# Strassen's scheme for half of the gate and up projections, with attention slices emitted at a higher pace

## The chip, the cores and the metric

The kernel runs on one core of one Trainium2 chip. The metric is the device time of one execution in microseconds (us). The span, from the first to the last instruction in a profile, is about 1.8 us shorter than the time of the same execution. In the profile lines PE is TensorE, PEld its weight loads, DVE VectorE, ACT ScalarE, POOL GpSimd, and SPq the queue of SyncE. PSUM holds the sums that matmuls build up, in 8 tiles (banks) in this kernel; an evacuation copies such a tile out.

## The reference

The input is x, 2048 tokens by 1024. Two blocks follow each other, each with a residual and a layer norm before it: a local attention with 32 heads of 32 (each token looks at 8 tokens, two apart), and a gated feed-forward block without an activation function.

```python
h  = x + A(layernorm(x), wqkv, wo)
# B: D = 1024, F = 3584
g = einsum("bsd,df->bsf", layernorm(h), w_gate)
u = einsum("bsd,df->bsf", layernorm(h), w_up)
h2 = h + einsum("bsf,fd->bsd", g * u, w_down)
```

## The kernel before

The tokens are cut into four chunks of 512. TensorE does all projections in bf16. VectorE does the attention, which has no matmul in it: for each of 8 offsets it multiplies and adds tiles of 128x4096. The attention is a generator, cut into slices. The program feeds slices into VectorE's instruction stream at a pace that a counter sets: each TensorE group earns credit, each slice costs some.

```python
class Background:
    def step(self, us):
        self.now += us
        self.credit = min(self.credit + us * self.rate, 4.0)
        while self.credit > 0:
            ...                              # next slice of a ready generator
            self.credit -= got               # (cut)
    def finish(self, gen):                   # emit all that is left of it, now
        ...
```

The attention's output goes through memory to be transposed: VectorE leaves it in `oD`, a store puts it in `od`, and four loads bring it back as `oT`.

```python
        nc.gpsimd.dma_start(od[c].rearrange("c g d s -> (c g) d s"), oD[:])
        oT = att.tile([128, KO, 4, SUB], BF, tag="oT", name=f"oT{c}")
        for cp in range(4):
            nc.gpsimd.dma_start(oT[:, :, cp, :], od[c][cp].rearrange("(hg hl) d s -> (hl d) hg s", hl=4))
```

The output projection (`wo`) reads `oT`. The feed-forward block has gate and up (`ffn1`) and the down projection (`ffn2`, two halves of 512 output columns):

```python
    def mm_group(ps, wt, j, rhs):            # ps: a PSUM tile
        for ko in range(KO):                 # 8 matmuls of 128x512
            nc.tensor.matmul(ps[:], lhsT=wt[:, ko, bass.ts(j, 128)], rhs=rhs[:, ko, :], ...)

    def ffn1(c, lnT):                        # (cut: loads, tiles)
        for b in range(7):
            for j in range(4):
                mm_group(pg, wts["wg", c, b], j, lnT)
                nc.scalar.copy(gs[:], pg[:])
                mm_group(pu, wts["wu", c, b], j, lnT)
                nc.scalar.copy(us[:], pu[:])
                nc.vector.tensor_tensor(gs[:], gs[:], us[:], ALU.mult)
```

The order at the end of the program:

```python
    qkv(3, range(4), last=True)
    bg.finish(atts[0])
    bg.rate = 0.9
    nxt = wo_ln2(0)
    qkv(3, range(4, 6), last=True)
    start_attention(3)
    for c in range(NCH):
        lnT2, hs = nxt
        hT = ffn1(c, lnT2)
        if c + 1 < NCH:
            bg.finish(atts[c + 1])
            nxt = wo_ln2(c + 1)              # output projection and layer norm
        ffn2(c, hT, hs)
```

## Time and profile before

| | kernel before |
|---|---|
| time, first three runs | 821.02, 824.99, 826.96 us |
| span of the profiled run | 817.9 us |
| TensorE busy | 99%, granted clock 1.00 |
| VectorE busy | 58%, but 81 to 98% in each stage from 20 us until the attention ends at 500 us |
| pace of a 128x512 bf16 matmul | 215.8 ns |
| attention of chunk 3 leaves VectorE | 499.85 us |
| its output projection starts | 607 us |

TensorE is the bound; the lines that show this stand in the prediction.

### The profile page before, as it was taken

To read this page: it belongs to the slowest core of one execution; us is meant where nothing else is said; L and a number is where in the kernel's file an instruction comes from. 1 tells how busy PE (TensorE), PEld (TensorE's weight loads), DVE (VectorE), ACT (ScalarE), POOL (GpSimd) and SP (SyncE) were. 2 spreads that over 40 slices of the span, in tenths; PEclk is the share of its full clock that TensorE was granted. 3 is DMA by queue.
4 is the path that set the end of the run, shared out by engine and by line. 5 is a ranking of instruction groups with operands and counts; after the bars stand their busy time and mean duration, and the time that the engine had idled before them with its cause. 6 is when DMAs were issued, how large, how long until landed. Compare 5 with 4: busy or idle time off the path is not lost.

```text
span 817.9 us, 9732 instructions
## 1 busy us (share of the span) xinstructions
PE 806.0 (99%) x3808; PEld 373.7 (46%) x3881; DVE 470.5 (58%) x520; ACT 222.4 (27%) x505; POOL 31.2 (4%) x60
## 2 busy tenths in 40 slices
PE   7999999999999999999999999999999999999998
PEld 5444444444444444444444444444444444444445
DVE  4539999998888899968887995111124111111011
ACT  2545444323333310023333000333320003333100
POOL 3100000200000200000200002000000000000000
PEclk9999999999999999999999999999999999999999
DMA  9999864999845969755863688636456753535400
GB/s 309 318 207 241 160 192 114 260 265 276 283 135 169 289 174 305 241 168 185 272 215 123 126 263 269 206 109 198 150 179 160 229 188 125 185 117 170 146 26 26
DMA packets 194494, 158.98 MB, mean 194 GB/s; under 512 B 83472, under 2 KB 188048, under 8 KB 192400
## 3 DMA queue, kind: packets, MB, share of 16 engines
q1 hardware_dynamic: 189904, 133.19, 57.4%
q0 software_dynamic: 4544, 25.17, 9.2%
q8 instruction: 30, 0.49, 0.3%
q14 instruction: 16, 0.13, 0.1%
HBM read 128.97 MB, written 22.02 MB: 185 GB/s over the span
## 4 chain that ended last, share of the span: by engine, by line
PE 97%; DMA 1%; issue 1%; SPq 0%; DVE 0%; ACT 0%
PE pg L330 24%; PE pu L330 24%; PE acc L512 21%; PE ps L330 19%; PE wo L453 7%; PE accl L502 3%; DMA x<-in_A_x_dram 1%; SPq L213 0%; PE ps L297 0%; SPq L221 0%; PE pt L288 0%; ACT lnT L289 0%; DVE ln L170 0%; DVE h L493 0%; DVE lnT L292 0%
## 5 line engine op out<-in xcount | busy, mean ns | idle before, releaser
L330 PE MATMUL pg<-lnT,w_wg 128*128 128x512 bf16 x879 | 210.1, 379 | 0.9
L330 PE MATMUL pu<-lnT,w_wu 128*128 128x512 bf16 x877 | 209.8, 379 | 0.9
L512 PE MATMUL acc<-w_wd,gs 128*128 128x512 bf16 x768 | 169.0, 379 | 0.8
L484 DVE TENSOR_TENSOR gs<-gs,us 128x512 bf16<-128x512 bf16 x112 | 47.4, 423 | 198.7 <-ACT us L483 198.7
L330 PE MATMUL ps<-lnT,w_qkv 128*128 128x512 bf16 x721 | 158.4, 379 | 0.8
L330 PEld LDWEIGHTS <-w_wg 128*128 128x128 bf16 x896 | 87.7, 98 | 105.7
L330 PEld LDWEIGHTS <-w_wu 128*128 128x128 bf16 x896 | 87.7, 98 | 105.7
L478 ACT CAST gs<-pg 128x512 bf16<-128x512 f32 x112 | 65.6, 586 | 235.9 <-PE pg L330 231.4
L512 PEld LDWEIGHTS <-gs 128*128 128x128 bf16 x784 | 76.7, 98 | 92.5
L330 PEld LDWEIGHTS <-w_qkv 128*128 128x128 bf16 x736 | 72.0, 98 | 86.6
L483 ACT CAST us<-pu 128x512 bf16<-128x512 f32 x112 | 65.6, 586 | 123.8 <-PE pu L330 114.6
L249 ACT CAST sg<-ps 128x512 bf16<-128x512 f32 x96 | 55.4, 586 | 63.8 <-PE ps L330 58.7
L415 DVE TENSOR_TENSOR pv<-vD,at 128x4096 bf16<-128x4096 bf16 x32 | 72.4, 2287 | 0.4
L375 DVE TENSOR_TENSOR prod<-qD,kD 128x4096 bf16<-128x4096 bf16 x32 | 72.3, 2285 | 0.1
L493 DVE TENSOR_TENSOR h<-acc,h 128x512 bf16<-128x512 f32 x28 | 17.4, 683 | 78.4 <-PE acc L512 78.4
L453 PE MATMUL wo<-w_wo,oT 128*128 128x512 bf16 x251 | 55.6, 379 | 0.3
L453 PEld LDWEIGHTS <-oT 128*128 128x128 bf16 x256 | 25.1, 98 | 30.2
L377 DVE TENSOR_TENSOR prod<-prod 128x4096 bf16<-128x4096 bf16 x16 | 36.6, 2289 | 0.3
L165 ACT ACTIVATE rs<-mv,eps 128x1 f32<-128x1 f32 x32 | 9.4, 294 | 75.7 <-DVE mv L162 70.8
L423 DVE TENSOR_TENSOR pv<-pv 128x4096 bf16<-128x4096 bf16 x12 | 27.5, 2289 | 0.2
L425 DVE TENSOR_TENSOR oD<-oD,pv 128x4096 bf16<-128x4096 bf16 x12 | 27.4, 2287 | 0.2
L502 PE MATMUL accl<-w_wd,gs 128*128 128x512 bf16 (+1 forms) x139 | 24.4, 336 | 0.1
(56 smaller groups left out, 291.3 us busy)
## 6 DMA issues: line engine op xcount, KB each, us to landing
w_wg<-in_B_w_gate_dram SPq DMA_DIRECT2D x28, 1024.0 KB, 7.0
w_wu<-in_B_w_up_dram SPq DMA_DIRECT2D x28, 1024.0 KB, 5.4
w_wd<-in_B_w_down_dram SPq DMA_DIRECT2D x32, 896.0 KB, 6.2
w_wo<-in_A_wo_dram SPq DMA_DIRECT2D x8, 1024.0 KB, 6.8
kd<-sg SPq DMA_DIRECT2D x32, 144.0 KB, 3.0
vd<-sg SPq DMA_DIRECT2D x32, 144.0 KB, 3.7
kD<-kd POOLq DMA_DIRECT2D x4, 1152.0 KB, 7.7
vD<-vd POOLq DMA_DIRECT2D x4, 1152.0 KB, 11.1
```

What stands on the lines that cost most here:

```text
L249: nc.scalar.copy(sg[:, HB:HB + TC], ps[:])
L330: nc.tensor.matmul(ps[:], lhsT=wt[:, ko, bass.ts(j, 128)], rhs=rhs[:, ko, :], start=(ko == 0), stop=(ko == KO - 1))
L375: nc.vector.tensor_tensor(prod[:, j], qD[:], kD[:, :, o:o + SUB], ALU.mult)
L377: nc.vector.tensor_tensor(prod[:, :, 0:16], prod[:, :, 0:16], prod[:, :, 16:32], ALU.add)
L415: nc.vector.tensor_tensor(pv[:, j], vD[:, :, o:o + SUB], at[:, w, None, :].to_broadcast((128, DH, SUB)), ALU.mult)
L423: nc.vector.tensor_tensor(pv[:, 0], pv[:, 0], pv[:, 1], ALU.add)
L453: nc.tensor.matmul(ps[:], lhsT=oTs[c][:, kk, t, :], rhs=wts["wo", c, hf][:, kk, :], start=(kk == 0), stop=(kk == KO - 1))
L478: nc.scalar.copy(gs[:], pg[:])
L483: nc.scalar.copy(us[:], pu[:])
L484: nc.vector.tensor_tensor(gs[:], gs[:], us[:], ALU.mult)
L502: nc.tensor.matmul(acc[:], lhsT=hT[f][:, bass.ts(t, 128)], rhs=wts["wd", c, hf, f // 7][:, f % 7, bass.ds(lo, n)], start=(f == 0), stop=(f ...
L512: nc.tensor.matmul(acc[t][:], lhsT=hT[f][:, bass.ts(t, 128)], rhs=wts["wd", c, hf, b][:, j, :], start=(f == 0), stop=(f == NF - 1))
```

## The change

The intent is to save matmuls. Chunks 2 and 3 are projected together, so that each pair of weight tiles meets a 2x2 arrangement: two halves of the contraction by two chunks. One level of Strassen's scheme (in Winograd's form) does this with 7 products in place of 8, for sums of weights and activations that other engines form. The sums are written as float32r, a four-byte type. Since chunks 2 and 3 are now needed together, chunk 3's attention has to be done much earlier, so its pace goes from 0.9 to 0.98.

```diff
+F32R = mybir.dt.float32r
...
+    def weight_sums(n, i):                       # GpSimd, per block and matrix
+        sw = wpool.tile([128, 4, 4, 128], F32R, tag="w", name=f"sw_{n}_{i}")
+        nc.gpsimd.tensor_tensor(sw[:, 0], a21, a22, ALU.add)
+        nc.gpsimd.tensor_tensor(sw[:, 1], sw[:, 0], a11, ALU.subtract)
+        nc.gpsimd.tensor_tensor(sw[:, 2], a11, a21, ALU.subtract)
+        nc.gpsimd.tensor_tensor(sw[:, 3], a12, sw[:, 1], ALU.subtract)
+        nc.scalar.copy(wc[:], a22)
...
+    def activation_sums(l2, l3):                 # once, on VectorE
+        nc.vector.tensor_tensor(t1[:], b12, b11, ALU.subtract)
+        ...
+    def product(ps, lhs, rhs, fresh):
+        for ko in range(4):
+            nc.tensor.matmul(ps[:], lhsT=lhs[:, ko, :], rhs=rhs[:, ko, :], start=(fresh and ko == 0),
+                             stop=(ko == 3), skip_group_check=not fresh)
...
+        for i in gu:                             # pair_block: gate and up (cut: PSUM tiles)
+            product(xb[i], wt[:, 0:4, i, 0:128], b11, True)      # bf16
+            nc.scalar.copy(yb[i][:], xb[i][:])                   # PSUM to PSUM
+        for i in gu:
+            product(vb[i], sw[i][:, 0], t1, True)                # float32r
+            nc.scalar.copy(p5[i][:], vb[i][:])
+            product(yb[i], sw[i][:, 1], t2, False)               # float32r
+            nc.scalar.copy(zb[i][:], yb[i][:])
+        for i in gu:
+            product(zb[i], sw[i][:, 2], t3, False)               # float32r
+            nc.vector.tensor_tensor(out[i][3], zb[i][:], p5[i][:], ALU.add)
+            product(xb[i], wt[:, 4:8, i, 0:128], b21, False)     # bf16
+            nc.scalar.copy(out[i][0], xb[i][:])
+        for i in gu:
+            product(zb[i], pair["c", n, i], t4, False)           # float32r
+            nc.scalar.copy(out[i][2], zb[i][:])
+            product(yb[i], sw[i][:, 3], bc, False)               # float32r
+            nc.vector.tensor_tensor(out[i][1], yb[i][:], p5[i][:], ALU.add)
+        for k in (3, 0, 2, 1):
+            nc.vector.tensor_tensor(out[0][k], out[0][k], out[1][k], ALU.mult)
...
-    bg.rate = 0.9
+    bg.rate = 0.98
...
+    hT = ffn1(1, lnT2)
+    bg.finish(atts[2])
+    l2, hs2 = wo_ln2(2)
+    h3 = att.tile([128, 4, D], BF, tag="qD", name="h3")          # residual of chunk 3
+    nc.sync.dma_start(h3[:], x[bass.ts(3, TC), :].rearrange("(t p) d -> p t d", p=128))
+    ffn2(1, 0, hT, hs)
+    bg.finish(atts[3])
+    l3, hs3 = wo_ln2(3)
+    activation_sums(l2, l3)                                      # (cut: loads, first weight_sums)
+    ffn2(1, 1, hT, hs, {0: lambda: weight_sums(0, 1)})
+    for n in range(NP):                                          # 14 blocks (cut)
+        pair_block(n, h23[4 * n:4 * n + 4])
+    # then the down projections of chunks 2 and 3
```

More of the change, by code (lines that the diff above doesn't have):

```diff
@@ L28 @@
 NF = F // 128
+NP = NF // 2
 EPS = 1e-5
@@ L127, with stream_wo, stream_wd @@
         stream.append((("qkv", b), wqkv_v[:, :, bass.ts(b, 512)], KO))
-    for c in range(NCH):
+    def stream_wo(c):
         for hf in range(2):
             stream.append((("wo", c, hf), wo_v[:, :, bass.ts(hf, 512)], KO))
+    def stream_wd(c, hf):
+        for b in range(4):
+            stream.append((("wd", c, hf, b), wd_v[:, bass.ts(b, 7), bass.ts(hf, 512)], 7))
+    for c in range(2):
+        stream_wo(c)
         if c > 0:
-            for hf in range(2):
-                for b in range(4):
-                    stream.append((("wd", c - 1, hf, b), wd_v[:, bass.ts(b, 7), bass.ts(hf, 512)], 7))
+            stream_wd(0, 0)
+            stream_wd(0, 1)
         for b in range(7):
@@ L137 @@
             stream.append((("wu", c, b), wu_v[:, :, bass.ts(b, 512)], KO))
-    for hf in range(2):
-        for b in range(4):
-            stream.append((("wd", NCH - 1, hf, b), wd_v[:, bass.ts(b, 7), bass.ts(hf, 512)], 7))
+    stream_wo(2)
+    stream_wd(1, 0)
+    stream_wo(3)
+    stream_wd(1, 1)
+    pair_at = len(stream)
+    for c in (2, 3):
+        stream_wd(c, 0)
+        stream_wd(c, 1)
     wts = {}
-    state = {"next": 0, "live": 0}
+    state = {"next": 0, "live": 0, "limit": pair_at}
     def pump(eng=None):
-        while state["next"] < len(stream) and state["live"] < 7:
+        while state["next"] < state["limit"] and state["live"] < 7:
             key, src, n = stream[state["next"]]
@@ L494, in ffn2_store @@
         nc.sync.dma_start(outf[bass.ds(c * TC + t * 128, 128), cols], hs[t][:, cols])
-    def ffn2(c, hT, hs):
-        for hf in range(2):
-            if c == NCH - 1 and hf == 1:
-                for t, lo, n in ((0, 0, 512), (1, 0, 512), (2, 0, 512), (3, 0, 256), (3, 256, 256)):
-                    acc = psum.tile([128, n], F32, tag="mm", name=f"accl{t}_{lo}")
-                    for f in range(NF):
-                        nc.tensor.matmul(acc[:], lhsT=hT[f][:, bass.ts(t, 128)],
-                                         rhs=wts["wd", c, hf, f // 7][:, f % 7, bass.ds(lo, n)],
-                                         start=(f == 0), stop=(f == NF - 1))
-                    ffn2_store(c, t, hf, acc, hs, lo, n)
-                continue
-            acc = [psum.tile([128, 512], F32, tag="mm", name=f"acc{c}_{hf}_{t}") for t in range(4)]
-            for b in range(4):
-                for j in range(7):
-                    f = b * 7 + j
-                    for t in range(4):
-                        nc.tensor.matmul(acc[t][:], lhsT=hT[f][:, bass.ts(t, 128)],
-                                         rhs=wts["wd", c, hf, b][:, j, :],
-                                         start=(f == 0), stop=(f == NF - 1))
-                    bg.step(0.86)
-                retire()
-            for t in range(4):
-                ffn2_store(c, t, hf, acc[t], hs)
-                bg.spend(0.7)
@@ new lines, in ffn2 @@
+    def ffn2(c, hf, hT, hs, between={}):
+        if c == NCH - 1 and hf == 1:
+            for t, lo, n in ((0, 0, 512), (1, 0, 512), (2, 0, 512), (3, 0, 256), (3, 256, 256)):
+                acc = psum.tile([128, n], F32, tag="mm", name=f"accl{t}_{lo}")
+                for f in range(NF):
+                    nc.tensor.matmul(acc[:], lhsT=hT[f][:, bass.ts(t, 128)],
+                                     rhs=wts["wd", c, hf, f // 7][:, f % 7, bass.ds(lo, n)],
+                                     start=(f == 0), stop=(f == NF - 1))
+                ffn2_store(c, t, hf, acc, hs, lo, n)
+            return
+        acc = [psum.tile([128, 512], F32, tag="mm", name=f"acc{c}_{hf}_{t}") for t in range(4)]
+        for b in range(4):
+            for j in range(7):
+                f = b * 7 + j
+                for t in range(4):
+                    nc.tensor.matmul(acc[t][:], lhsT=hT[f][:, bass.ts(t, 128)],
+                                     rhs=wts["wd", c, hf, b][:, j, :],
+                                     start=(f == 0), stop=(f == NF - 1))
+                bg.step(0.86)
+            retire()
+            if b in between:
+                between[b]()
+        for t in range(4):
+            ffn2_store(c, t, hf, acc[t], hs)
+            bg.spend(0.7)
@@ new lines, with load_pair @@
+    pair = {}
+    def load_pair(n):
+        wt = wpool.tile([128, KO, 2, 256], BF, tag="w", name=f"w_pair_{n}")
+        for i, src in enumerate((wg_v, wu_v)):
+            nc.sync.dma_start(wt[:, :, i, :], src[:, :, bass.ts(n, 256)])
+        pair["w", n] = wt
+        state["live"] += 1
+    def weight_sums(n, i):
+        wt = pair["w", n]
+        a11, a12 = wt[:, 0:4, i, 0:128], wt[:, 4:8, i, 0:128]
+        a21, a22 = wt[:, 0:4, i, 128:256], wt[:, 4:8, i, 128:256]
+        sw = wpool.tile([128, 4, 4, 128], F32R, tag="w", name=f"sw_{n}_{i}")
[3 more added lines that the diff above has]
+        nc.gpsimd.tensor_tensor(sw[:, 3], a12, sw[:, 1], ALU.subtract)
+        wc = lnp.tile([128, 4, 128], F32R, tag="ln", name=f"wc_{n}_{i}")
+        nc.scalar.copy(wc[:], a22)
+        pair["s", n, i], pair["c", n, i] = sw, wc
+        state["live"] += 1
@@ new lines, in activation_sums @@
+    def activation_sums(l2, l3):
+        b11, b12, b21, b22 = l2[:, 0:4, :], l3[:, 0:4, :], l2[:, 4:8, :], l3[:, 4:8, :]
+        t1 = att.tile([128, 4, TC], F32R, tag="kD", name="t1p")
+        t2 = att.tile([128, 4, TC], F32R, tag="vD", name="t2p")
+        t34 = att.tile([128, 2, 4, TC], F32R, tag="prod", name="t34p")
+        bc = att.tile([128, 4, TC], F32R, tag="oD", name="bcp")
+        nc.scalar.copy(bc[:], b22)
+        nc.vector.tensor_tensor(t1[:], b12, b11, ALU.subtract)
+        nc.vector.tensor_tensor(t2[:], b22, t1[:], ALU.subtract)
+        nc.vector.tensor_tensor(t34[:, 0], b22, b12, ALU.subtract)
+        nc.vector.tensor_tensor(t34[:, 1], b21, t2[:], ALU.subtract)
+        pair["b"] = (b11, b21, t1, t2, t34[:, 0], t34[:, 1], bc)
@@ new lines, in product, with pair_block, bank @@
+    def product(ps, lhs, rhs, fresh):
+        for ko in range(4):
+            nc.tensor.matmul(ps[:], lhsT=lhs[:, ko, :], rhs=rhs[:, ko, :], start=(fresh and ko == 0),
+                             stop=(ko == 3), skip_group_check=not fresh)
+    def pair_block(n, hts):
+        b11, b21, t1, t2, t3, t4, bc = pair["b"]
+        wt = pair["w", n]
+        gu = range(2)
+        sw = [pair["s", n, i] for i in gu]
+        out = [hts, [t1k.tile([128, TC], BF, tag="t1k", name=f"up{n}_{k}")[:] for k in range(4)]]
+        def bank(k, i):
+            return psum.tile([128, TC], F32, tag="mm", name=f"p{k}{n}_{i}")
+        xb, yb, zb, vb, p5 = [[None] * 2 for _ in range(5)]
+        for i in gu:
+            xb[i] = bank("x", i)
+            product(xb[i], wt[:, 0:4, i, 0:128], b11, True)
+            yb[i] = bank("y", i)
+            nc.scalar.copy(yb[i][:], xb[i][:])
+        for i in gu:
+            vb[i] = bank("v", i)
+            product(vb[i], sw[i][:, 0], t1, True)
+            p5[i] = att.tile([128, TC], F32, tag=("lg", "t3")[i], name=f"p5{n}_{i}")
+            nc.scalar.copy(p5[i][:], vb[i][:])
+            product(yb[i], sw[i][:, 1], t2, False)
+            zb[i] = bank("z", i)
+            nc.scalar.copy(zb[i][:], yb[i][:])
[11 more added lines that the diff above has]
+            nc.vector.tensor_tensor(out[0][k], out[0][k], out[1][k], ALU.mult)
+        state["live"] -= 3
@@ L541 @@
     start_attention(3)
-    for c in range(NCH):
-        lnT2, hs = nxt
-        hT = ffn1(c, lnT2)
-        if c + 1 < NCH:
-            bg.finish(atts[c + 1])
-            nxt = wo_ln2(c + 1)
-        ffn2(c, hT, hs)
+    lnT2, hs = nxt
+    hT = ffn1(0, lnT2)
+    bg.finish(atts[1])
+    nxt = wo_ln2(1)
+    for hf in range(2):
+        ffn2(0, hf, hT, hs)
+    lnT2, hs = nxt
+    hT = ffn1(1, lnT2)
[3 more added lines that the diff above has]
+    nc.sync.dma_start(h3[:], x[bass.ts(3, TC), :].rearrange("(t p) d -> p t d", p=128))
+    hss[3] = [h3[:, t, :] for t in range(4)]
+    ffn2(1, 0, hT, hs)
+    bg.finish(atts[3])
+    l3, hs3 = wo_ln2(3)
+    activation_sums(l2, l3)
+    load_pair(0)
+    load_pair(1)
+    weight_sums(0, 0)
+    ffn2(1, 1, hT, hs, {0: lambda: weight_sums(0, 1)})
+    h23 = [t1k.tile([128, TC], BF, tag="t1k", name=f"hq{i}")[:] for i in range(24)]
+    for i in range(4):
+        ht = hp.tile([128, D], BF, tag="h", name=f"hq_h{i}")
+        h23 += [ht[:, 0:TC], ht[:, TC:2 * TC]]
+    for ht in (att.tile([128, KO, TC], BF, tag="oT", name="hq_o"),
+               lnTp.tile([128, KO, TC], BF, tag="lnT", name="hq_l"), l3):
+        h23 += [ht[:, k, :] for k in range(KO)]
+    for n in range(NP):
+        if n + 1 < NP:
+            weight_sums(n + 1, 0)
+            weight_sums(n + 1, 1)
+            if n + 2 < NP:
+                load_pair(n + 2)
+        else:
+            state["limit"] = len(stream)
+            pump()
+        pair_block(n, h23[4 * n:4 * n + 4])
+    pump()
+    for c, hs in ((2, hs2), (3, hs3)):
+        hT = [h23[2 * f + c - 2] for f in range(NF)]
+        for hf in range(2):
+            ffn2(c, hf, hT, hs)
 _INS = ['A_x', 'A_wqkv', 'A_wo', 'B_x', 'B_w_gate', 'B_w_up', 'B_w_down']
```

## The prediction

> **What bounds the kernel now.** I read the page first, for the bound and the clock.
>
> ```profile
> PE 806.0 (99%) x3808; PEld 373.7 (46%) x3881; DVE 470.5 (58%) x520; ACT 222.4 (27%) x505; POOL 31.2 (4%) x60
> ...
> PEclk9999999999999999999999999999999999999999
> ...
> PE 97%; DMA 1%; issue 1%; SPq 0%; DVE 0%; ACT 0%
> ...
> L330 PE MATMUL pg<-lnT,w_wg 128*128 128x512 bf16 x879 | 210.1, 379 | 0.9
> L330 PE MATMUL pu<-lnT,w_wu 128*128 128x512 bf16 x877 | 209.8, 379 | 0.9
> ...
> L484 DVE TENSOR_TENSOR gs<-gs,us 128x512 bf16<-128x512 bf16 x112 | 47.4, 423 | 198.7 <-ACT us L483 198.7
> L330 PEld LDWEIGHTS <-w_wg 128*128 128x128 bf16 x896 | 87.7, 98 | 105.7
> L478 ACT CAST gs<-pg 128x512 bf16<-128x512 f32 x112 | 65.6, 586 | 235.9 <-PE pg L330 231.4
> ```
>
> TensorE is busy 99% of the span at the full clock, the chain that ended last is 97% TensorE, and its idle time before the gate and up matmuls is 0.9 us in each row. So the time is the count of matmuls times their pace. The 379 ns in the rows are overlapped lengths; the pace comes from the timeline of TensorE, which I read second:
>
> ```profile
> 448.22 13.98 PE L453 MATMUL wo<-w_wo,oT 128*128 128x512 bf16 x63
> 462.04 48.51 PE L512 MATMUL acc<-w_wd,gs 128*128 128x512 bf16 x219
> 510.38 1.89 PE L330 MATMUL pg<-lnT,w_wg 128*128 128x512 bf16 x8
> ```
>
> The output projection of chunk 2 is 64 matmuls (one record is missing) and takes 462.04 - 448.22 = 13.82 us, so one 512-column matmul costs 215.9 ns; the down projection gives 48.34/224 = 215.8 ns. A weight load of 98 ns hides under that.
>
> Third, I read where the last attention ends, because the change needs it sooner (timelines of VectorE and GpSimd):
>
> ```profile
> 497.56 2.29 DVE L425 TENSOR_TENSOR oD<-oD,pv 128x4096 bf16<-128x4096 bf16 x1
> 509.94 2.48 DVE L493 TENSOR_TENSOR h<-acc,h 128x512 bf16<-128x512 f32 x4 [10.08 <-PE acc L512]
> ...
> 501.00 0.57 POOL L427 DMA_DIRECT2D od<-oD  x1 [105.86 <-issue]
> 506.78 3.54 POOL L430 DMA_DIRECT2D oT<-od  x4 [5.21 <-DMA od<-oD]
> ```
>
> Attention of chunk 3 leaves VectorE at 497.56 + 2.29 = 499.85, is stored, and its four transposed loads are issued from 506.78. Today nobody needs it until 607, where the output projection of chunk 3 starts.
>
> **What the Trainium skill says.**
> - "TensorE: Matmul & The Clock Gate", section "Wait — 56ns, not 53.3ns?": N/2.4 GHz plus about 2.5 ns, 215.7 ns at 512 columns. The trace's 215.8 agrees.
> - "FP8 and Floating Point Precision", section "TensorE Precision Notes": reduced-precision FP32 reads four bytes and truncates to FP22, whereas true FP32 takes four passes. I read this as one pass for the new float32r matmuls. The trace has none, so it is untested here.
> - "SBUF — State Buffer", section "A bandwidth-pool intuition that's wrong (but worth ruling out)": the moving-operand path is put at about 614 GB/s, two bytes per lane at 2.4 GHz. Taken literally, a four-byte stream would run at half pace. Also untested here, and my main doubt.
> - "GPSIMD Engine Reference", section 3.1: about 2.6 cycles per element for a two-input operation. For 512 elements at 1.2 GHz that makes 1.1 us (an estimate from that page). The trace has no such GpSimd instruction.
>
> **The change, part by part.**
>
> *Removed on the path.* Gate and up of chunks 2 and 3 are now 2 chunks x 28 tiles x 2 x 8 = 896 matmuls. After: 14 blocks x 2 matrices x 7 products x 4 = 784, of 128x512 as before. The 112 fewer give 112 x 215.8 ns = 24.2 us, 2.9% of 825. Of the 784, 560 (five products in seven) are float32r. If they go at bf16 pace, a block of 56 takes 12.1 us and all blocks 169.2 us, against 193.4.
>
> *Added beside it, per block of 12.1 us.* ScalarE: 10 evacuations or PSUM copies and two weight copies, about 12 x 0.59 = 7.0 us. VectorE: 4 sums from PSUM (the down projection's like sum takes 0.68) and 4 products of 0.42: 4.4 us. GpSimd: 8 sums of 512 elements, 8 x 1.1 to 1.3 = 9 to 10.5 us, the tightest. Weights: 1 MB, about 85 GB/s, where 1 MB took 7.0 us to land with rows twice as long. Each is below 12.1.
>
> *Waits inside a block.* In product slots of 0.86 us the order is x0 x1 v0 y0 v1 y1 z0 x0 z1 x1 z0 y0 z1 y1. The copy of x0 to y0 starts after slot 1 and is wanted at slot 4; the copy of y0 to z0 starts after slot 4 and is wanted at slot 7. Each has some 1.7 us for a copy of about 0.6. All 8 banks are used, but the next block's y0 bank, freed last but one, is wanted only a slot after that block begins. I see no steady wait. Weight sums of block n+1 can begin about when block n does and are wanted 1.7 us into block n+1, so GpSimd needs only its throughput.
>
> *Moved.* The output projection of chunk 3 now comes after the first half of chunk 1's down projection, at 462.0 + 24.2 = 486.2. Attention must be done, stored and reloaded by then, hence the rate of 0.98. In the gate and up stage a pair of groups gives 0.9 x 3.46 - 0.45 = 2.66 of credit now, 0.98 x 3.46 - 0.45 = 2.94 after, 10% more; one attention costs 82.9. I summed the counter over the program's steps and laid VectorE's instructions end to end with the trace's durations. For before this gives ends of attention 2 and 3 at 387.3 and 500.5 (trace: 386.1 and 499.9); after, 366.5 and 475.0, with VectorE never more than 3.2 us behind TensorE. Store and reload in before took, from VectorE's end, 6.9 us to the first reload's issue (499.85 to 506.78), then 4.5 to 9.8 us to land. So the first slice is there at 475.0 + 5.5 to 7 + 4.5 to 8 = 485 to 490: a stall of 0 to 4 us, I take 2.
>
> *Once.* The activation sums (four 128x2048 VectorE operations, about 2.3 us each from the 1.22 us of a 1024-element one) and the first GpSimd sums fall under the second half of chunk 1's down projection, 24.2 us of TensorE work: hidden. The down projections of chunks 2 and 3 are only moved.
>
> *Sum.* 825.0 - 24.2 + 2 (late attention) + 2 (float32r overhead and block seams, a choice: 3 to 4 ns per float32r matmul) = 804.8, so 805.
>
> **The rivals.**
> - *Float32r streams or loads slower.* Each extra 10 ns on 560 matmuls costs 5.6 us; an extra 43 ns eats the whole gain (24.2/560); half pace costs 560 x 215.8 = 121 us, and the kernel lands near 922. A weight load left exposed at its 98 ns costs 55 us, near 856. For it: the moving-path figure, and that four-byte weights are twice the bytes. Against it: the one-pass wording, and that a kernel tuned this closely would hardly have kept a scheme of halved pace.
> - *GpSimd becomes the bound.* Eight sums at 1.5 us make 12.1 us. At 1.8 us a block takes 14.4 us and the gain is gone: 14 x 2.3 = 32 us, about 837. VectorE's work on two SBUF inputs is light here (1.7 us per block), which speaks against much contention.
> - *The late attention.* A reload as slow as 9.8 us, after a store of 8.7, stalls some 8 us: 811, within 2%.
> - *VectorE too full at rate 0.98*, so that evacuations hold TensorE: at 0.9 it is 81 to 99% busy until 486. With 8 banks (some 12 us of groups) a lag of 3 us should cost nothing. In the worst case 3 to 5 us.
> - *Weights of a block land late*, and ScalarE, which copies them in order, then holds the PSUM copies: more than about 12 us to land would be needed.
>
> **Range and chances.** The certain term is 24.2 us; the 2% line is at 808.5, so losses may reach 7.7 us. I expect about 4, with a tail to the slow side: range 798 to 822. Clearly faster 0.65; within 2% (a longer stall, or 10 to 25 ns more per float32r matmul) 0.22; slower by over 2% (half pace, an exposed load, GpSimd) 0.13.
>
> **What would show it.** Right: TensorE's idle before the chunk 3 output projection under 4 us; a block every 12.1 to 12.4 us, from the starts of the bf16 x products; GpSimd sums near 1.2 us; no wait of TensorE on ScalarE or GpSimd; full granted clock. Wrong: a block of 13 us or more with TensorE busy throughout (then float32r is the cause), or with waits on GpSimd or ScalarE in it; a stall near 486 us of over 6 us; gaps of TensorE before that, which would charge the rate.

## The result, and the profile after

| | before | after |
|---|---|---|
| median time | 823.00 us (820.36 to 826.96, 4 runs) | 813.76 us (813.69 to 814.85, 4 runs) |
| span of the profiled run | 817.9 | 812.0 |
| mean granted clock | 1.000 | 0.995 |

The ratio is 0.9887, with a 95% interval of 0.984 to 0.9934: a small gain, inside the 2% that counts as the same. A ratio here is the mean time of one kernel's fast runs over that of the other's of the same rounds, so it is not quite the ratio of the medians in the table. The result is correct.

First the page of the changed kernel: busy times, then the clock in 40 slices, then the chain that ended last by engine.

```profile
PE 795.3 (98%) x3700; PEld 410.6 (51%) x3769; DVE 551.8 (68%) x580; ACT 254.9 (31%) x562; POOL 171.8 (21%) x172
...
PEclk9999999999999999999999998999999999999999
...
PE 83%; issue 13%; DMA 3%; SPq 0%; POOL 0%; DVE 0%; ACT 0%; POOLq 0%
```

TensorE is still the bound, but one slice of the clock is below full, and a transfer (DMA) now has 3% of the chain. (Most of the 13% of "issue" is no lost time of TensorE: the chain runs back through GpSimd's store of attention 3, and the profile shows no wait for the 97.5 us before that store.) Slice 25 is near 490 us. The timeline of TensorE shows what happened there (start, length, engine, line, instruction, count, and in brackets the idle time before and what ended it):

```profile
448.44 13.98 PE L466 MATMUL wo<-w_wo,oT 128*128 128x512 bf16 x63
462.26 24.34 PE L524 MATMUL acc<-w_wd,gs 128*128 128x512 bf16 x109
491.47 16.78 PE L466 MATMUL wo<-w_wo,oT 128*128 128x512 bf16 x63 [4.88 <-DMA oT<-od]
508.09 24.34 PE L524 MATMUL acc<-w_wd,gs 128*128 128x512 bf16 x110
```

TensorE idles 4.88 us for the reload of attention 3. The projection after it then takes 508.09 - 491.47 = 16.62 us, where the same work for chunk 2 took 13.82: 2.80 us more, at a granted clock of 0.83 over this stretch. So the late attention costs 7.7 us, of which the idle time is only the larger part.

VectorE and GpSimd around it:

```profile
472.75 2.29 DVE L438 TENSOR_TENSOR oD<-oD,pv 128x4096 bf16<-128x4096 bf16 x1
...
476.19 0.56 POOL L440 DMA_DIRECT2D od<-oD  x1 [97.51 <-issue]
485.90 3.54 POOL L443 DMA_DIRECT2D oT<-od  x4 [9.15 <-DMA od<-oD]
```

Attention left VectorE at 472.75 + 2.29 = 475.04; the prediction's sum said 475.0. But store and reload took from there to 491.47, 16.4 us, where the prediction allowed 10 to 15. The excess is in the store: 10.9 us from VectorE's end to the first reload's issue at 485.90, where 5.5 to 7 had been allowed. The 5.6 us from there to TensorE's start lie inside the 4.5 to 8 allowed.

Now one block of the scheme, again in the timeline of TensorE. `px` are the bf16 products (two for each of gate and up), all others are float32r (the trace calls it f32):

```profile
545.09 1.90 PE L575 MATMUL px<-lnT,w_pair 128*128 128x512 bf16 x8
546.64 1.29 PE L575 MATMUL pv<-t1p,sw 128*128 128x512 f32 x4
547.76 1.10 PE L575 MATMUL py<-t2p,sw 128*128 128x512 f32 x4
548.70 1.09 PE L575 MATMUL pv<-t1p,sw 128*128 128x512 f32 x4
549.63 1.10 PE L575 MATMUL py<-t2p,sw 128*128 128x512 f32 x4
550.56 1.09 PE L575 MATMUL pz<-t34p,sw 128*128 128x512 f32 x4
...
557.93 1.90 PE L575 MATMUL px<-lnT,w_pair 128*128 128x512 bf16 x8
```

A block takes 557.93 - 545.09 = 12.84 us, not 12.08, with no idle time in it. From one float32r product to the next (547.76, 548.70, 549.63, 550.56) is 0.933 us for four matmuls: 233.3 ns each, 17.5 ns more than bf16. Over 560 matmuls that is 9.8 us, and the fourteen blocks together lose 14 x 0.755 = 10.6 us; the remaining 0.8 us is left for the changes between types and is not much more than the reading error.

With that the spans add up: 817.9 - 24.2 (112 matmuls fewer) + 10.6 (float32r) + 4.9 (idle) + 2.8 (slow clock) = 812.0, which is the span measured. The helpers did not hold TensorE: GpSimd's eight sums took about 8 x 1.28 = 10.3 us per block.

### The profile page after: what moved, and what is told of

It is laid out like the page before. It is cut to its first block, busy times and chain, and to the rows that moved or that the text cites. A ratio compares the mean times of both kernels' runs of the same rounds, so it can differ in the third digit from the quotient of the medians.

```text
span 812.0 us, 9901 instructions
## 1 busy us (share of the span) xinstructions
PE 795.3 (98%) x3700; PEld 410.6 (51%) x3769; DVE 551.8 (68%) x580; ACT 254.9 (31%) x562; POOL 171.8 (21%) x172
## 4 chain that ended last, share of the span: by engine, by line
PE 83%; issue 13%; DMA 3%; SPq 0%; POOL 0%; DVE 0%; ACT 0%; POOLq 0%
PE ps L343 19%; PE acc L524 18%; PE pg L343 7%; PE pu L343 7%; PE pz L575 6%; PE py L575 6%; PE px L575 6%; PE wo L466 5%; PE pv L575 3%; PE accl L514 3%; DMA od<-oD 1%; DMA x<-in_A_x_dram 1%; DMA oT<-od 1%; POOL oT L443 0%; SPq L226 0%
## 5 line engine op out<-in xcount | busy, mean ns | idle before, releaser
L343 PE MATMUL pg<-lnT,w_wg 128*128 128x512 bf16 x439 | 105.0, 379 | 0.5
L343 PE MATMUL pu<-lnT,w_wu 128*128 128x512 bf16 x439 | 104.9, 379 | 0.4
L524 PE MATMUL acc<-w_wd,gs 128*128 128x512 bf16 x439 | 96.7, 379 | 0.5
L524 PEld LDWEIGHTS <-gs 128*128 128x128 bf16 x448 | 43.9, 98 | 52.8
L343 PEld LDWEIGHTS <-w_wg 128*128 128x128 bf16 x448 | 43.8, 98 | 52.9
L343 PEld LDWEIGHTS <-w_wu 128*128 128x128 bf16 x448 | 43.8, 98 | 52.9
L491 ACT CAST gs<-pg 128x512 bf16<-128x512 f32 x56 | 32.8, 586 | 91.5 <-PE pg L343 88.1
L575 PE MATMUL px<-lnT,w_pair 128*128 128x512 bf16 x210 | 52.5, 380 | 0.9
L496 ACT CAST us<-pu 128x512 bf16<-128x512 f32 x56 | 32.8, 586 | 60.1 <-PE pu L343 54.4
L551 POOL TENSOR_TENSOR sw<-w_pair 128x512 fp32r<-128x512 bf16 x28 | 36.5, 1302 | 60.5 <-issue 32.2
L553 POOL TENSOR_TENSOR sw<-w_pair 128x512 fp32r<-128x512 bf16 x28 | 36.9, 1318 | 0.0
```

Source lines behind the costliest of these rows:

```text
L524: nc.tensor.matmul(acc[t][:], lhsT=hT[f][:, bass.ts(t, 128)], rhs=wts["wd", c, hf, b][:, j, :], start=(f == 0), stop=(f == NF - 1))
L551: nc.gpsimd.tensor_tensor(sw[:, 0], a21, a22, ALU.add)
L553: nc.gpsimd.tensor_tensor(sw[:, 2], a11, a21, ALU.subtract)
L575: nc.tensor.matmul(ps[:], lhsT=lhs[:, ko, :], rhs=rhs[:, ko, :], start=(fresh and ko == 0), stop=(ko == 3), skip_group_check=not fresh)
```

## The experiments

The theory after the result has two parts. First, the pace of the blocks is that of four-byte operands and nothing else. Second, the stall at 486 us comes from how late attention leaves VectorE and from crowded queues, and the slow clock follows from the stall. The rivals are that the scheme's order of products costs the time, that the weight load sets the pace, and that the faster pace of attention itself slows TensorE. All ten runs gave correct results. The kernel before ran beside them: in eight runs 820.64 us was the median. The changed kernel was not run again beside them. Against the kernel before, e1, e3 and e4 are each faster, but their intervals reach across the 2% line, so their verdict is "unclear"; e7, e8 and e10 are clear of it.

### e1: sums in float16

```diff
-F32R = mybir.dt.float32r
+F32R = mybir.dt.float16
```

> All sums of weights and activations are written as float16 (two bytes, 10 mantissa bits) in place of float32r; nothing else changes. My theory: a block takes 12.84 us because each of its 40 float32r matmuls starts 233.3 ns after the one before, against 215.8 for bf16, and it is the four-byte operands that cost the 17.5 ns. Then every matmul of the block comes at 215.8 ns, a block takes 56 x 0.2158 = 12.1 us, and the span falls by 14 x 0.75 = 10.5 us, to about 801.5 (time about 803). Rival: the extra 0.75 us per block comes from the order of the products (hand-overs of PSUM banks, accumulating onto copied sums). Then a block stays at 12.8 and the time at 813. The stall before the output projection of chunk 3 (4.9 us idle, then 2.8 us of slowed clock) stays in either case. The result should still agree with the reference.

Measured: 804.25 us median (801.09 to 806.35, 4 runs), ratio to before 0.9779 (0.9715 to 0.9844); span of the profiled run 801.1. From the timeline of TensorE, two blocks follow each other like this:

```profile
543.92 1.89 PE L575 MATMUL px<-lnT,w_pair 128*128 128x512 bf16 x8
...
556.01 1.89 PE L575 MATMUL px<-lnT,w_pair 128*128 128x512 bf16 x8
...
557.74 1.03 PE L575 MATMUL pv<-t1p,sw 128*128 128x512 f16 x4
558.60 1.03 PE L575 MATMUL py<-t2p,sw 128*128 128x512 f16 x4
```

A block takes 556.01 - 543.92 = 12.09 us, and four float16 matmuls 0.86 us. The order of products, the banks and the copies are unchanged, so that rival is out: the whole 10.6 us belongs to the four-byte type. The stall was still there in this run (5.08 us idle).

### e2: each float32r matmul in two halves

```diff
+        halves = 2 if lhs.dtype == F32R else 1
+        n = TC // halves
         for ko in range(4):
-            nc.tensor.matmul(ps[:], lhsT=lhs[:, ko, :], rhs=rhs[:, ko, :], ...)
+            for h in range(halves):
+                nc.tensor.matmul(ps[:, bass.ts(h, n)], lhsT=lhs[:, ko, :], rhs=rhs[:, ko, bass.ts(h, n)], ...)
```

> Each float32r matmul of 512 moving columns is split in two of 256 columns, each with its own weight load; bf16 matmuls stay whole. This asks what sets the 233.3 ns. Columns stream slower (0.456 ns each): the halves come every 117 ns, the block stays at 12.84 us. A fixed addition per matmul of 17 to 20 ns: every 124 to 129 ns, block 13.4 to 13.8 us. The float32r weight load (188 ns in the trace, against 98) sets the pace: every 188 to 233 ns, block 18.5 to 22.1 us, span up by 79 to 130 us. My theory is the last, at 233; by the first a float32r operand is simply streamed at a lower pace.

Measured: one run, 815.83 us, span 814.1. My theory missed here. The timeline of TensorE:

```profile
548.68 1.10 PE L578 MATMUL py<-t2p,sw 128*128 128x256 f32 x8
549.62 1.10 PE L578 MATMUL pv<-t1p,sw 128*128 128x256 f32 x8
550.57 1.11 PE L578 MATMUL py<-t2p,sw 128*128 128x256 f32 x8
551.51 1.11 PE L578 MATMUL pz<-t34p,sw 128*128 128x256 f32 x8
```

Eight halves take 0.943 us, 118 ns each, with a weight load for every one. If the load set the pace at 233 ns, halving the columns could not bring it to 118, and a fixed addition per matmul would have given 124 to 129. A block takes 12.93 us (546.00 to 558.93), against 12.84. The cost goes with the columns: the second 256 columns of a whole matmul add 233.3 - 118 = 115 ns, 0.45 ns a column, against 0.42 (215.8/512) for bf16. The group of weight loads does show longer records (188 ns for float32r, 98 for bf16; 189 in this run, longer than the 118 between matmuls), but they are hidden. This is one profile, and the comparison lies within it, so its unknown state does not matter here.

### e3: pace 1.00

```diff
-    bg.rate = 0.98
+    bg.rate = 1.0
```

> The pace of attention is 1.00 in place of 0.98; nothing else changes. By the same sum that gave 475.0 for the end of attention 3 on VectorE (the trace: 475.04) it now ends near 470. My theory: the 4.9 us idle of TensorE before the output projection of chunk 3 is the late store and reload, and the slower clock after it (16.6 in place of 13.8 us for that projection) follows from the idle time. Then the idle falls to 0 to 1 us, the projection takes 13.8 us, and the span falls by 6.5 to 7.7 us, to 804.5 to 805.5 (time about 806.5). Rival 1: the store and the reload are held by the DMA queue and not by VectorE, so the reload still lands near 491: no gain. Rival 2: the clock drop has another cause (the change of load): only 4.9 us come back. Rival 3: VectorE is too full, TensorE gets gaps before 448.

Measured: 807.63 us median, ratio 0.9837 (0.9778 to 0.9897). Three of the four runs have spans of 805.6, 805.7 and 806.1 at a clock of 1.000, within 0.6 us of the forecast, which fits idle time and slow clock both being gone; these runs have no profile. The profiled run is the other one, with a span of 812.2. Its timeline shows another stall of the same kind, at the output projection of chunk 0, whose store took 8.15 us:

```profile
169.56 16.56 PE L466 MATMUL wo<-w_wo,oT 128*128 128x512 bf16 x63 [3.60 <-DMA oT<-od]
...
494.40 13.99 PE L466 MATMUL wo<-w_wo,oT 128*128 128x512 bf16 x63 [0.94 <-DMA oT<-od]
```

The part of the program up to here is the same in the kernel before. 3.60 us of idle time and 185.96 - 169.56 = 16.40 in place of 13.82 us make 6.2 us. That is about the distance between the two groups of runs of the kernel before (820 and 826). No slow run of that kernel was profiled, so this explanation of its spread is an inference. At chunk 3, idle time of 0.94 us cost no clock: both losses there are gone in this profile.

### e4: the residual of chunk 3 loaded earlier

```diff
     hT = ffn1(1, lnT2)
+    h3 = att.tile([128, 4, D], BF, tag="qD", name="h3")
+    nc.sync.dma_start(h3[:], ...)
+    hss[3] = [h3[:, t, :] for t in range(4)]
     bg.finish(atts[2])
     l2, hs2 = wo_ln2(2)
-    h3 = ...                                    # the same lines, moved up
```

> The 1 MB load of the residual of chunk 3 is issued before the output projection of chunk 2 (near 446) in place of after it (470); the pace stays 0.98. In the changed kernel the store of attention 3 took 9.1 us to land, against 4.2 to 8.7 before, with this load and three weight tiles in the queues just ahead of it. Theory: the crowding by this load is what made the store late; it lands in 5 to 6.5 us, the idle falls from 4.9 to 1 to 2.5 us, and with less than that idle the clock drop is gone too: span down by 3 to 6 us. Rival: the weight tiles alone fill the queues, the store still takes 8 to 9 us and the span falls by under 1 us.

Measured: 809.94 us median (808.19 to 814.60, 4 runs), ratio 0.9856 (0.9799 to 0.9912). GpSimd's and TensorE's timelines in the profiled run, which was the quickest one:

```profile
476.09 0.56 POOL L440 DMA_DIRECT2D od<-oD  x1 [97.34 <-issue]
485.10 3.54 POOL L443 DMA_DIRECT2D oT<-od  x4 [8.45 <-DMA od<-oD]
...
488.67 13.99 PE L466 MATMUL wo<-w_wo,oT 128*128 128x512 bf16 x63 [2.18 <-DMA oT<-od]
```

This is a half-hit. The idle time fell to 2.18 us and the clock stayed full, so the span is 806.4. But the store was hardly quicker (476.09 to 485.10, against 476.19 to 485.90); it was the reload that came 2.0 us sooner (3.57 in place of 5.57 us from its issue to TensorE's start). Nor is the quicker reload shown to come from the early load: over the profiles at pace 0.98 or 1.00 with a stall at chunk 3 that time lies between 3.6 and 7.5 us, and it was 7.5 in e7 (below), which has the early load too. So crowding by this load explains at most a small part of the slow store. Two of the other three runs gained less, and one (814.60) nothing.

### e5: the kernel before at pace 0.98

```diff
-    bg.rate = 0.9
+    bg.rate = 0.98
```

> The kernel before with the second part of the change alone: pace 0.98 in place of 0.9. Theory: attention is off TensorE's path there, so nothing moves: attention 3 leaves VectorE near 475 in place of 500, TensorE has no new gaps, span 818 plus or minus 1. Rival: a fuller VectorE delays evacuations and TensorE loses 1 to 5 us between 165 and 448, a cost that the changed kernel carries too.

Measured: two runs at 820.35 and 820.58 us, two at 826.17 and 827.32; ratio 1.0026 (0.9956 to 1.0096). The profiled run has a span of 818.6 and no gap between 165 and 448. Alone, the faster pace gains nothing and costs nothing that these runs can show.

This run also answers a question of e4. GpSimd issued the store of attention 3 at 476.64, close to where the changed kernel does, and its reload waited for it as long:

```profile
485.54 3.54 POOL L430 DMA_DIRECT2D oT<-od  x4 [8.34 <-DMA od<-oD]
```

The scheme and its load of chunk 3's residual are not in this kernel. So neither is needed to make this store slow.

### e6: the changed kernel at pace 0.9

```diff
-    bg.rate = 0.98
+    bg.rate = 0.9
```

> The changed kernel with the first part alone: the pace back at 0.9. By the sums of the prediction attention 3 leaves VectorE near 500 where the output projection of chunk 3 is wanted at 486. With the 16 us that store and reload took in the changed kernel (475.0 to 491.5) TensorE idles to about 515: 29 us idle, some 3 us of slowed clock, span 812 + 24 = about 836 to 840: the scheme alone would lose. Rival: the stall of the changed kernel is set by the DMA queues and not by when attention ends; then the idle stays near 5 us and the span near 812.

Measured: one run, 831.57 us, span 829.8.

```profile
509.87 16.14 PE L466 MATMUL wo<-w_wo,oT 128*128 128x512 bf16 x63 [22.90 <-DMA oT<-od]
...
501.60 0.56 POOL L440 DMA_DIRECT2D od<-oD  x1 [105.88 <-issue]
506.33 3.53 POOL L443 DMA_DIRECT2D oT<-od  x4 [4.16 <-DMA od<-oD]
```

The scheme alone loses to the kernel before, as expected, and the rival (a stall that does not depend on when attention ends) is out. The span forecast, 836 to 840, was 6 to 10 us too high, though: the store was issued at 501.60, as forecast, but landed so soon that the reload was issued 4.7 us later and TensorE started 8.3 us after the store's issue, in place of 15.3 in the changed kernel (491.47 - 476.19). The 40 slices of DMA activity say what else was moving, first in the changed kernel (475 to 492 us), then in this run (500 to 511 us):

```profile
DMA  9999999997599999999989999999999999999999
DMA  0000000002899999879000000000097675959999
```

In the changed kernel the store shared the 16 DMA engines with weight loads, at 357 GB/s in all; here nothing but the store and its reload moved. Over all profiles the store of attention 3 took 8.0 to 9.2 us in the nine at pace 0.98 or 1.00, where it is issued between 471 and 478, and 4.2 to 5.4 us in the three at 0.9, where it is issued at 501 or later. So its length goes with the place in the program. That the other traffic is what makes it slow fits the two rows, but it is not shown: in the kernel before the queues moved 303 GB/s from 500 to 516 us, and the store still took only 5.2 us.

### e7 and e8: the findings together

e7 is e1, e3 and e4 in one kernel. e8 also moves the output projection of chunk 0 one block of the qkv projection later:

```diff
-    qkv(3, range(4), last=True)
+    qkv(3, range(5), last=True)
     bg.finish(atts[0])
     bg.rate = 1.0
     nxt = wo_ln2(0)
-    qkv(3, range(4, 6), last=True)
+    qkv(3, range(5, 6), last=True)
```

> The changed kernel with float16 sums, pace 1.00 and the early residual load together. Theory: the two losses are independent and both go: 817.9 - 24.2 = 793.7 for the span, plus 0 to 1.5 of remaining idle: 793.7 to 795.2, time about 796; runs in which the reload of attention 0 is late (as in the profiled run at pace 1.00: 3.6 us idle at 166 and a slowed projection after it) lie 5 to 7 us higher. Rival: with blocks of 12.1 us GpSimd, at 10.3 us of sums per block, or the weight transfers begin to hold TensorE: block over 12.2 us.

> The same, and the output projection of chunk 0 one block of the qkv projection (6.9 us) later, so that the reload of attention 0 has that much more time. Theory: the slow runs of all these kernels, the one before included (826 to 827 against 820), are the late reload of attention 0; then all runs lie within 2 us, at 795 to 797. Rival: they have another cause, and one run in three is still 5 to 7 us longer. Risk: the last normalisation and its transpose now have 6.9 us in place of 13.8 before the gate projection of chunk 0 needs them; a gap of 0 to 2 us could open there.

Measured: e7 797.18 us median (795.83 to 802.54, 6 runs), ratio 0.9709 (0.9658 to 0.976); e8 797.95 us (797.38 to 799.12, 6 runs), ratio 0.9704 (0.9667 to 0.9741). In e7's profiled run (span 794.8) a block takes 12.09 us and the idle time at chunk 3 is 0.98 us: both losses are gone and no helper has become a bound. Two of its runs are longer (800.23 and 802.54). In e8 all six lie within 1.8 us, as forecast, though at 797.4 to 799.1 and not at 795 to 797. Its profile has a store of attention 0 that was slow again (8.63 us to land) and cost nothing, at the price of the gap that had been forecast:

```profile
195.32 1.89 PE L343 MATMUL pg<-lnT,w_wg 128*128 128x512 bf16 x7 [1.91 <-DMA lnT<-ln]
```

### e9: the same move in the kernel before

The edit is the diff of e8, applied to the kernel before.

> The kernel before, with the output projection of chunk 0 one qkv block (6.9 us) later and nothing else. In all, 3 of the 11 runs of the kernel before so far lie at 826 to 827.3 and most others near 820.5. Theory: the slow ones are runs in which the reload of attention 0 is late. Then with this edit all runs lie within 2 us of each other, at 822 to 823 (820.5 and the 1.9 us gap before the gate projection that the same move opened in the combined kernel), and none at 826. Rival: another cause; about one run in three is still some 6 us longer than the rest.

Measured: five runs at 821.28 to 822.67 us and one at 828.25; ratio 1.0014 (0.9975 to 1.0053). The one slow run was the profiled one, and it shows no stall at the output projection:

```profile
172.33 13.98 PE L453 MATMUL wo<-w_wo,oT 128*128 128x512 bf16 x64
186.14 7.07 PE L330 MATMUL ps<-lnT,w_qkv 128*128 128x512 bf16 x32
198.56 3.57 PE L330 MATMUL pg<-lnT,w_wg 128*128 128x512 bf16 x8 [5.35 <-DMA lnT<-ln]
```

Here the late transfer is the transpose of the last normalised tile, which this edit had made tight: 5.35 us idle, and then eight matmuls in 3.57 us, where they usually take 1.89. The move trades one tight transfer for another. It neither proves nor refutes that the slow runs of the kernel before are late reloads: one slow run in six, with a cause of its own, says too little beside 3 in 11 (825.29 to 826.18) of the kernel before.

### e10: half a block later

This is e7 with the output projection of chunk 0 moved by two of a block's four groups.

```diff
     qkv(3, range(4), last=True)
+    qkv(3, [4], groups=range(2))
     bg.finish(atts[0])
     ...
-    qkv(3, range(4, 6), last=True)
+    qkv(3, [4], last=True, groups=range(2, 4))
+    qkv(3, [5], last=True)
```

> The combined kernel (float16 sums, pace 1.00, early residual load) with the output projection of chunk 0 half a qkv block (3.45 us) later. Theory: the late reload cost 3.6 us of idle and then 2.7 us of slowed clock; half a block covers the idle but for 0 to 1 us, and the 10.4 us left for the last normalisation leave no gap before the gate projection. All runs at 795.5 to 797.5. Rival: the store can be later still, and one run in six is at 800 or more; or a gap of 1 us or more opens before the gate projection.

Measured: 797.07 us median (794.80 to 799.90, 6 runs), ratio 0.9707 (0.9671 to 0.9743). The best run has a span of 793.0 and no gap of TensorE after the start-up; that is 817.9 - 24.2 = 793.7 within the noise, so all of the 24.2 us was had there. The spread is 5 us, wider than the 2 us forecast, and the medians of e7, e8 and e10 cannot be told apart. These versions beat both kernels: about 2.9% under the kernel before, beside which they ran, and some 2% under the changed kernel.

## Why the prediction was right or wrong

The range held (813.76 in 798 to 822). The most likely class did not: "clearly faster" had 0.65, and the outcome was "the same", at 0.22. By its own steps:

- **The saving on the path** was right: 784 matmuls in 14 blocks of 56, and 24.2 us, as e7 and e10 show once the losses are gone.
- **"I see no steady wait" in a block, and helpers below 12.1 us:** right. The blocks have no idle time, with float16 a block takes 12.09 us, and the forecast of 9 to 10.5 us for GpSimd met 10.3. VectorE's 4.4 us were too few: it was busy for 7.4 us of the block shown, because its four products took 1.23 us each in place of 0.42 (the contention that the prediction thought small, see the last section). It stayed off TensorE's path.
- **"3 to 4 ns per float32r matmul":** wrong in size. It is 17.5 ns (e1, e2), so the term of about 2 us is 10.6. The rival "streams or loads slower" was named and priced (10 ns, 5.6 us); its form was slower streaming, and neither half pace nor an exposed load.
- **"A stall of 0 to 4 us, I take 2":** wrong in size and incomplete. When attention ends was right to 0.1 us. The error was in the store, 10.9 us from VectorE's end to the reload where 5.5 to 7 had been allowed. The prediction read this from attention 3 of the kernel before, at a place in the program where the store is quick (e6); attention 1 of the same trace waited 8.7 us for its store, and that figure went into the rival "the late attention" alone, which put the time at 811. The second error was in the consequence: after 4.9 us without work TensorE's clock fell, and that cost 2.8 us more. So the term of 2 us is 7.7.
- **That consequence was there to be read.** The Trainium skill, "TensorE: Matmul & The Clock Gate", section "Why this matters for your kernels", asks for no idle gaps over about 3 us between bursts of matmuls, or the clock halves. The runs agree: gaps of 3.60, 4.88, 5.08, 5.35, 5.45 and 22.90 us were followed by slow matmuls at a granted clock of 0.50, gaps of 0.94, 0.98, 1.91 and 2.18 us were not. But 3 us is no safe length: in e3 the clock fell 2.0 us after TensorE went idle, in the changed kernel 3.7 us and in e2 4.5 us after. The prediction looked up the page for the pace of matmuls and left this out.
- **"VectorE too full at rate 0.98":** did not happen (e5), nor at 1.00 (e3). The 81 to 99% that the prediction read are 81 to 97% by its stage windows up to 486 us; nothing hangs on it.
- **The signs it named:** the block (12.84 us, named right up to 12.4 and wrong from 13) and the stall (4.88 us, right below 4, wrong above 6) fell between its two lists. No wait on a helper and GpSimd sums near 1.2 us came true; the full granted clock did not (0.995).
- **The sum** started from 825.0, the median of three runs of which two lie in the upper group. With 820.6, the median of the eight runs beside e1 to e8, and the true terms, 820.6 - 24.2 + 10.6 + 7.7 = 814.7 (measured: 813.76). Part of the prediction's nearness to the result was luck: this high start hid 4.4 us of its two errors.

What stays open: what makes the 1 MB store slow at one place and quick at another, why the store of attention 0 took 5.5 to 5.9 us in ten profiles and over 8 in two (e3, e8), and which of its two operands slows a float32r matmul, since they were not mixed with two-byte ones here.

## What to carry to other kernels

A fast algorithm has to keep the pace of the unit it saves work on: here 7 products in place of 8 save 12.5%, and an operand type that is 8% slower in five of the seven gave back 44% of it (10.6 of 24.2 us). When work is moved ahead, count the whole path to its user: the slowest store and load seen, and not those of the place that the work is moved away from; and, if TensorE may idle for more than some 2 us, the slowed clock after it as well. Check too whether a time at the start of a sum is one state of the kernel or a mixture of two.

## What the Trainium skill lacked or had wrong

- "TensorE: Matmul & The Clock Gate", section "Why this matters for your kernels": gaps over about 3 us are to be avoided; in e3 the clock fell 2.0 us into a gap. The half clock then lasted about 6.8 us in the five cases with gaps of 3.6 to 5.5 us.
- The same page has no pace for float32r. The runs show 233.3 ns for 512 columns and 118 ns for 256, against 215.8 ns for bf16 and float16 at 512; the weight load's record is 188 ns in place of 98 and stays hidden.
- "SBUF — State Buffer" puts the moving-operand path at about 614 GB/s for bf16. That is no limit for four-byte operands: 128 x 512 x 4 bytes in 233.3 ns are 1,124 GB/s, if all four bytes are read.
- "GPSIMD Engine Reference", section 3.1, leads to 1.1 us for a sum of 512 elements, and the runs show 1.15 us alone. It gives no figure for such a sum beside VectorE, where the changed kernel shows 2.85 to 3.20 us (during the activation sums), and VectorE's own products of two bf16 tiles in the blocks went from 423 to 1229 ns. In the last two blocks, when GpSimd has no sums left, they are back at 418 ns:

```profile
517.68 2.85 POOL L551 TENSOR_TENSOR sw<-w_pair 128x512 fp32r<-128x512 bf16 x1 [28.25 <-DMA w_pair<-in_B_w_gate_dram]
526.82 1.15 POOL L554 TENSOR_TENSOR sw<-w_pair,sw 128x512 fp32r<-128x512 bf16 x1
...
L613 DVE TENSOR_TENSOR hq<-hq,up 128x512 bf16<-128x512 bf16 x24 | 28.1, 1229 | 0.0
L613 DVE TENSOR_TENSOR lnT<-lnT,up 128x512 bf16<-128x512 bf16 x8 | 2.8, 418 | 0.0
```
